# Speech codec kernel, one core: two halo rows copied instead of loaded, x by two eight-row transposes a chunk, fewer DMA adds, three small copies and two updates on other engines

## The chip, the cores and the metric

One core of a Trainium2 chip runs the whole program. The metric is device microseconds of one execution, as the median of three runs. Beside the runs stands one profiled execution, whose trace is read below.

## What is computed

The input x is 2 sequences of 16,000 tokens with 512 channels, in bf16. The reference, cut to what matters:

```python
z = sum over i of xp[:, i:i+T, :] * dw_enc[i]      # 3 taps along the tokens, x padded by one row
z = silu(z)
res = z; q = zeros_like(z)
for s in range(4):                                  # 4 stages, 8 code words each
    cb = codebooks[s]
    d2 = |res|^2 - 2 * res @ cb.T + |cb|^2
    sel = cb[d2.argmin(-1)]
    q = q + sel
    res = res - sel
y = sum over i of qp[:, i:i+T, :] * dw_dec[i]      # 3 taps again
```

So every token needs itself and its two neighbours, then four rounds of "score against 8 words, take the least, subtract the word", and the output is made from the words chosen for a token and its neighbours.

## The kernel before

The 32,000 tokens are dealt over 128 partitions: partition p holds 250 consecutive tokens. Column g of that grid is one "group" of 128 tokens. The 250 groups are worked in 17 chunks, one of 12 groups, thirteen of 16, then 12, 12 and 6 (padded to 8). Within a chunk channels stand on the partitions: x comes in transposed, as the tile XT of 128 channels by (groups + 2) by 4 channel blocks by 128 tokens.

A chunk passes through three parts:

- **Front** (`front`, and `load` ahead of it). `load` brings XT in with DMA transposes on SyncE's queue (L507), four rows (groups) a DMA. A chunk of 16 groups needs 18 rows, because the taps reach one group to either side; so it takes five DMAs, of 4, 4, 4, 4 and 2 rows, and neighbouring chunks load two rows twice. XT has two buffers. For each of the four channel blocks i, VectorE multiplies by the three taps (`product`, L578) into the tiles Z, T1 and T2; then T1 and T2 are added to Z (`total`). An addition is either a VectorE instruction (L586) or an accumulating DMA that GpSimd issues (L584); the table `DMA_ADDS` says which. The result goes through SiLU: exp on ScalarE (L590), plus one on VectorE (L594), reciprocal on ScalarE (L599), a product on VectorE into the residual RES (L606).
- **Four stages** (`stage`). TensorE scores RES against the words (L680, with a mask at L672). VectorE reduces the scores to a maximum that holds the token's norm (L700), ScalarE copies out the products (L706), and four VectorE instructions (L733 to L748) find the least distance and mark it in OH. TensorE turns the marks (L759), the turned marks are copied from PSUM to the tile MT, TensorE expands them (L784) and ScalarE cuts them into PH (L793). The table `TURNED` says who makes the MT copy: VectorE in the first three stages (L775), ScalarE in the fourth (L773). Then the word is taken off RES, channel block by channel block. Either TensorE makes the chosen word (`chosen`, L822) and VectorE adds it (`subtract`, L832), or TensorE makes the whole new residual in PSUM (`rest`, L838 and L843) and ScalarE copies it back in two halves (`keep`, L850). The table `ON_DVE` gives, for each chunk and stage, how many of the four blocks take VectorE's way.
- **Finish** (`finish`, `outputs`). TensorE multiplies the marks with tables of words times taps (L886), ScalarE copies the rows out of PSUM into YSB (L896), and SyncE's queue stores them, four groups a DMA (L899). YSB has two buffers.

Three chunks are in work at a time (RES has three buffers). The order of everything is a plan: each piece of work is a task with an engine, a holding time, a delay, needs and buffers, and the string `RANKS` gives each task its start in the plan, by which the instructions are emitted; `PLACES` gives the PSUM banks. The engines then run their queues strictly in that order, each waiting on semaphores.

One rule is written by hand: transposes and accumulating DMAs take turns. `keep_apart` makes each transpose wait for the last add but one that was emitted before it, and each add for the last transpose but one (`LAG = 2`).

```python
    def keep_apart(t, mine, others):
        if len(others) >= LAG:
            tc.add_manual_dep(t.ins, others[-LAG].name, mybir.DependencyInfo(mybir.DependencyClass.Sync, mybir.DependencyReason.DATA),
                              reason="transposes and adds take turns")
        mine.append(t.ins)
```

So SyncE's queue, which holds transposes and stores in one order, can stand at a transpose until an add has landed, with stores behind it; GpSimd's queue can stand at an add until a transpose has landed.

Of the kernel before, what the change touches and what calls it, by code (L numbers as in the profile page):

```python
# [18 lines left out]
J = 4  # L19
# [10 lines left out]
TURNED = (0, 0, 0, 1)  # L30

ON_DVE = [(3, 3, 3), (3, 3, 3), (3, 3, 3), (3, 3, 3), (3, 2, 3), (3, 3, 3), (3, 2, 3), (3, 3, 3), (3, 2, 3), (3, 3, 3), (3, 2, 3), (3, 3, 3), (3, 2, 3), (3, 3, 3), (4, 4, 4), (4, 4, 4), (4, 4, 4)]
# [5 lines left out]
DMA_ADDS = [((), ())] + [((0, 1, 2, 3), (2, 3))] * 16  # L38

RUN = 4  # L40
# [8 lines left out]
RANKS = ("0403020v1u1W0i1A0J0E0O0U0x0k3`4e4t4p4M4A523<0z001o1F1+1|1T1-1D1V5Q01121E1)1c252x01051G5]001!5$0f1Q1w5*0a1c1m5-1(1|2Y1-2]"  # L49
         "323Q2r2w2K2T2/3h3.22282i2d2B3w3U1]1=312*3g3L3)3!43404k4L4!4!4<4{5f5l575q5w5G5O5Z5(5+5[5^606A6J6b6m656d6q6Q6g6J6I6-6_7l6Y"  # L50
         "6?7k7x7F7S7#7&7;7>7_8b8r7~87858h8N8!8s8D8Z8>959c8*8^9b9i9l9n9t9w9D9F9Ma4ak9X9)9R9^9$9~agaxasaJa%a?aYa]b8bobMcvcWc(c=dod&"
         "d|d,d?eKf@g2d,eqfqgNgZeGeTiGe`fijkjC4d3p4o5j5v5I5;4`3C5f4,5{687c393Z3[3v4>6r6S4G3J4P5I5;6Z766?7m7n7H7G7%7Z7^8B8S8Y8g8z8K"
         "8X8+9d9j9m9q9v9y9E9J9R9`a9aqaLa9at9:a6axa,aLb7bwbLa[b4bsb0bkbrbZb*b<b|c0c5c8cfcAc!cucJclcxcTc*cHcVc*d0dednc>dadmdadwd%d."
         "d`d}eLeXe;e>fbfiftfpfGfIfUfPf$fwfKf$f[g4gng3ghgsgSg<hdhVh%h<h|ioiziFiWi$i`j5i-i@jojAj:jhjqjZk3jCjLjXjHjOj_khkRkuk!l4lm2:"
         "3S3q2:5H3c6Y6~7t8E8W8,9c7<6(7}6/8.9e9x7y6w7!8L8`9-a37V6C8q8}9safaFaEa-a@bababBbtbNb)b]b}b>c7ccb!b?b^ctcUcXc.c;c@dhdHeket"
         "d{e6dWd:dMeBd)e9eseMe(e]e*e^fge!e-e[fsfFfRf)g1g9gegng@h5gGgRg/g_g#g;gwgQg~hBhOh,hrhEh$hihzh%h{h~ibiriui.i=j0jsjGj9jnjBjR"
         "jTj)k0kskbk#k~l7kBkUl8lelslAlLlZl$l*l.m3mqmImOmVm:n#n>oSo&qjmPm&o1qBmOoDo@oeoromozp[n=n|pEq95P8R6h716O6=9M9Ga(9!cbcndTb+"
         "9=c6b!c]d4dqbpaWbAb}cCdodZa|9Tb9cmc&dLd(d*eiejeMe$e}e^fhgkg?hcf!f?glf:f_gthghphwhChLhThWh&i3ieiaiCihirh[i8h.h~iqi!i@i~iP"
# [54 lines left out]
LAG, SLACK, STORE = 2, 4.5, 0.35  # L113
# [61 lines left out]
def kernel(  # L175
# [318 lines left out]
    def load(st, org):  # L494
# [30 lines left out]
        def behind():  # L525
            nc.gpsimd.tensor_copy(st["XT"][0:1, 0, 0, 0:2], XR[0:1, 1, 0:2])
            nc.gpsimd.tensor_copy(st["XT"][0:1, 0, 0, 2:4], CB4[0:1, 0:2])
            for b in range(B):
                p = b * HB + 32
                nc.gpsimd.tensor_copy(st["XT"][p:p + 1, 0, 0, 0:2], XR[p:p + 1, 0, 0:2])  # L530
# [492 lines left out]
```

## Time and profile before

| what | value |
|---|---|
| median of 3 runs | 687.65 us (678.28 to 690.9) |
| the profiled execution, its own time | 681.25 us |
| its span, first to last instruction | 679.5 us |
| mean granted TensorE clock | 0.936 |
| VectorE busy | 605.9 us (89%) |
| ScalarE busy | 555.2 us (82%) |
| TensorE busy with matmuls | 537.8 us (79%) |
| DMA moved | 119.38 MB |

The profile's page gives for each engine the busy time, its share of the span and the number of instructions. DVE is VectorE, ACT ScalarE, PE TensorE (PEld its weight loads), POOL GpSimd, SP SyncE; a "q" behind a name is the engine's sequencer, which issues and waits. A group of instructions is named by line, engine, operation and tiles (out<-in); behind the bar stand its busy time, the mean of one in ns, and the idle time of the engine just before them with what ended it. A row of the view of waits reads: who waited, at which line, for whom, total us, number of waits, longest. The view of windows gives each engine's busy time within a stretch, then the granted clock, the DMA share (mean busy share of the 16 DMA engines; it can pass 1 where packets overlap) and GB/s.

### The profile page before, as it was taken

Reading aid. Unit: us, or ns where it says so; the run is one execution under the profiler, and the core shown is the slowest. Engines: PE = TensorE matmul, PEld = TensorE weight load, DVE = VectorE, ACT = ScalarE, POOL = GpSimd, SP = SyncE. Lnnn points to the kernel's source line nnn. Section 1 sums busy time; section 2 is a strip of 40 time slices with the busy share of each in tenths; the row PEclk is TensorE's granted clock in tenths of the full one; section 3 lists DMA queues with packets and bytes.
Section 4 is the critical chain, followed back from the end, with each engine's and each line's share of the span. In section 5 each row is a group of like instructions: output and inputs, shape, how many; then the busy total and the mean of one; then the engine's idle time right before and its main releaser. Section 6 shows DMA issues by size and latency. Waiting matters only on the chain.

```text
span 679.5 us, 25822 instructions
## 1 busy us (share of the span) xinstructions
PE 537.8 (79%) x11513; PEld 324.4 (48%) x11550; DVE 605.9 (89%) x1166; ACT 555.2 (82%) x675; POOL 102.1 (15%) x147
## 2 busy tenths in 40 slices
PE   4136686788888697887988979579879998899995
PEld 4123345355455444454454544345545555566661
DVE  5998999999999698998889999499979999999961
ACT  2567586979798699998899988499969889997586
POOL 8020203011212102020211102012120122110000
PEclk8657799989899799998999999899989999999998
DMA  8999899979999999999999997989979487362345
GB/s 166 161 181 193 145 174 179 187 157 166 242 223 178 154 213 180 229 175 184 224 185 210 167 249 137 130 211 184 204 152 184 118 155 187 88 163 91 127 170 204
DMA packets 164889, 119.38 MB, mean 176 GB/s; under 512 B 143801, under 2 KB 144186, under 8 KB 164650
## 3 DMA queue, kind: packets, MB, share of 16 engines
q1 hardware_dynamic: 150032, 69.88, 49.2%
q0 software_dynamic: 14464, 47.59, 38.7%
q8 instruction: 90, 1.47, 0.9%
q10 hardware_dynamic: 282, 0.26, 0.1%
q14 instruction: 21, 0.17, 0.1%
HBM read 2.36 MB, written 32.77 MB: 52 GB/s over the span
## 4 chain that ended last, share of the span: by engine, by line
DVE 40%; ACT 18%; PE 16%; DMA 15%; issue 9%; POOL 1%; SPq 0%; ACTq 0%; DVEq 0%; POOLq 0%
DVE RES L832 11%; DMA XT<-in_x_dram 8%; DVE T L578 6%; PE PS L680 6%; DVE TR L700 6%; DMA Z<-T 5%; DVE RES L606 5%; ACT E L599 5%; PE PS L822 4%; ACT E L590 4%; ACT YSB L896 4%; DVE E L594 3%; DVE Z L578 3%; ACT RES L850 2%; DVE Z L586 2%
## 5 line engine op out<-in xcount | busy, mean ns | idle before, releaser
L680 PE MATMUL PS<-RES 128*64 128x80 bf16 (+1 forms) x8064 | 177.1, 202 | 36.3 <-issue 25.4
L680 PEld LDWEIGHTS <-RES 128*64 128x64 bf16 x8064 | 171.5, 114 | 45.2 <-issue 26.7
L832 DVE TENSOR_TENSOR RES<-RES,PS 128x2048 bf16<-128x2048 bf16 (+2 forms) x202 | 175.6, 902 | 10.3 <-PE PS L822 9.8
L584 POOL DMA_DIRECT2D Z<-T x96 | 85.9, 944 | 498.8 <-DVE TR L700 70.7
L896 ACT ACTIVATE YSB<-PS 128x1024 bf16<-128x1024 f32 x126 | 124.0, 1031 | 13.6 <-PE PS L886 8.6
L590 ACT ACTIVATE E<-Z 128x2048 bf16<-128x2048 bf16 (+2 forms) x68 | 121.3, 1792 | 13.0 <-DVE Z L586 11.3
L599 ACT ACTIVATE E<-E 128x2048 bf16<-128x2048 bf16 (+2 forms) x68 | 121.7, 1799 | 1.1 <-DVE E L594 0.9
L700 DVE TENSOR_REDUCE TR<-PS 128x6 bf16<-128x384 f32 (+1 forms) x188 | 93.9, 509 | 17.4 <-PE PS L680 14.6
L578 DVE TENSOR_SCALAR T<-XT,WENC 128x2048 bf16<-128x2048 bf16 (+2 forms) x136 | 94.9, 710 | 11.9 <-DMA XT<-in_x_dram 10.7
L850 ACT ACTIVATE RES<-PS 128x1024 bf16<-128x1024 f32 x88 | 89.9, 1032 | 7.4 <-PE PS L843 6.9
L606 DVE TENSOR_TENSOR RES<-Z,E 128x2048 bf16<-128x2048 bf16 (+2 forms) x68 | 77.6, 1141 | 1.3 <-ACT E L599 1.3
L706 ACT ACTIVATE PR<-PS 128x48 bf16<-128x48 f32 (+1 forms) x188 | 36.0, 215 | 49.2 <-DVE TR L700 48.9
L822 PE MATMUL PS<-PH,HIGH 64*128 64x512 bf16 (+2 forms) x314 | 62.2, 381 | 12.2 <-ACT PH L793 4.2
L672 PE MATMUL PS<-MASK,IDENT 128*64 128x384 bf16 (+1 forms) x376 | 63.1, 327 | 11.0 <-ACT RES L850 4.6
L838 PE MATMUL PS<-RES,IDENT 128*128 128x512 bf16 (+1 forms) x188 | 58.1, 391 | 4.7 <-DVE RES L832 2.0
L822 PE MATMUL PS<-PH,LOW 64*128 64x512 bf16 (+2 forms) x314 | 59.7, 366 | 0.4 <-issue 0.4
L822 PE MATMUL PS<-PH,MID 64*128 64x512 bf16 (+2 forms) x314 | 59.7, 366 | 0.1
L886 PE MATMUL PS<-S,OHT 64*128 64x512 bf16 (+1 forms) x169 | 53.4, 397 | 6.1 <-DVE RES L832 2.7
L886 PE MATMUL PS<-T,OHT 64*128 64x512 bf16 (+1 forms) x170 | 51.9, 395 | 5.5 <-ACT OHT L790 1.8
L578 DVE TENSOR_SCALAR Z<-XT,WENC 128x2048 bf16<-128x2048 bf16 (+2 forms) x68 | 48.3, 710 | 5.6 <-DMA XT<-in_x_dram 5.3
L672 PEld LDWEIGHTS <-IDENT 128*64 128x64 bf16 x376 | 24.9, 109 | 44.5 <-issue 41.2
L586 DVE TENSOR_TENSOR Z<-Z,T 128x2048 bf16<-128x2048 bf16 (+2 forms) x40 | 44.2, 1112 | 0.8 <-DMA Z<-T 0.8
(109 smaller groups left out, 594.4 us busy)
## 6 DMA issues: line engine op xcount, KB each, us to landing
Z<-T POOLq DMA_DIRECT2D x78, 512.0 KB, 6.7
out_dram<-YSB SPq DMA_DIRECT2D x61, 512.0 KB, 4.6
Z<-T POOLq DMA_DIRECT2D x12, 384.0 KB, 5.8
RES<-in_x_dram SPq DMA_DIRECT2D x1, 1664.0 KB, 7.1
Z<-T POOLq DMA_DIRECT2D x6, 256.0 KB, 4.5
XT<-in_x_dram SPq DMA_TRANSPOSE x76, 6.4
out_dram<-YSB SPq DMA_DIRECT2D x1, 384.0 KB, 2.3
out_dram<-YSB SPq DMA_DIRECT2D x1, 256.0 KB, 2.6
```

Of the source, the lines that this page charges most:

```text
L578: nc.vector.tensor_scalar(out=places(u[name]), in0=taps(i, k), scalar1=WENC[:, i, k:k + 1], scalar2=None, op0=ALU.mult)
L590: nc.scalar.activation(u["E"][:, 0:G, :], u["Z"][:, 0:G, :], ACT.Exp, scale=-1.0)
L599: nc.scalar.add_instruction(mybir.InstActivation(func=ACT.Reciprocal, name=nc.get_next_instruction_name(), engine=mybir.EngineType.Activation,
L606: nc.vector.tensor_tensor(out=tokens(st["RES"], i, G), in0=halves(u["Z"]), in1=halves(u["E"]), op=ALU.mult)
L672: nc.tensor.matmul(both(V[d * HT:(d + 1) * HT], m, home, HT), lhsT=IDENT[:, d * HT:(d + 1) * HT], rhs=MASK[:, 0:m, :].rearrange("p (n o) t ...
L680: nc.tensor.matmul(V[d * HT:(d + 1) * HT, own - left:own + HT + right], lhsT=row[:, at:at + HT], rhs=row[:, at - left:at + HT + right], st ...
L700: nc.vector.tensor_reduce(out=to, in_=both(u["V", q], m, home, HT), axis=AX.X, op=ALU.max)
L822: nc.tensor.matmul(SEL[:, h, 0:W], lhsT=words[side(h), i * P:(i + 1) * P], rhs=u["PH"][side(h), :], start=(k == 0), stop=(k == len(parts) ...
L832: nc.vector.tensor_tensor(out=old, in0=old, in1=new, op=ALU.add)
L850: nc.scalar.activation(old, new.rearrange("p h (n t) -> p (h n) t", t=HT), ACT.Copy)
L886: nc.tensor.matmul(Y[:, h, :], lhsT=lhs()[rows], rhs=DEC[table][rows], start=(a == 0), stop=(a == len(banks[k][h][1]) - 1), skip_group_che ...
L896: nc.scalar.activation(u["YSB"][:, at:at + step * (n - 1) + 1:step, :], u[k][:, 0:n, :], ACT.Copy)
```

## The change

Five things change in the code, and the plan's tables are new throughout.

- `load`: rows 0 and 1 of XT are no longer loaded. A new task `halo` lets VectorE copy them from the last two rows of the XT of the chunk before (L535 of the changed kernel). `RUN` goes from 4 to 8, so a chunk of 16 groups takes two transposes of eight rows.
- The XT buffer used to come free with the last `product` of its chunk. Now a new task `released` frees it when that product and the next chunk's halo copy are both done.
- `DMA_ADDS`: in the even chunks from 2 to 16 the second addition of channel block 2 goes from DMA to VectorE. Of 96 accumulating DMAs 88 are left.
- `TURNED`: the MT copies of the first three stages, 51 of them, go from VectorE to ScalarE.
- `ON_DVE`: chunks 1, 3, 5, 7, 9, 11 and 13 have (3, 2, 3), before it was chunks 4, 6, 8, 10 and 12. So two more chunks have one more channel block that goes through `rest` and `keep`.

The holding times and delays that the plan gives to transposes, adds and stores are other numbers, too, and stand in the diff.

```diff
-TURNED = (0, 0, 0, 1)
+TURNED = (1, 1, 1, 1)
-ON_DVE = [(3, 3, 3), (3, 3, 3), (3, 3, 3), (3, 3, 3), (3, 2, 3), (3, 3, 3), (3, 2, 3), (3, 3, 3), (3, 2, 3), (3, 3, 3), (3, 2, 3), (3, 3, 3), (3, 2, 3), (3, 3, 3), (4, 4, 4), (4, 4, 4), (4, 4, 4)]
+ON_DVE = [(3, 3, 3), (3, 2, 3), (3, 3, 3), (3, 2, 3), (3, 3, 3), (3, 2, 3), (3, 3, 3), (3, 2, 3), (3, 3, 3), (3, 2, 3), (3, 3, 3), (3, 2, 3), (3, 3, 3), (3, 2, 3), (4, 4, 4), (4, 4, 4), (4, 4, 4)]
-DMA_ADDS = [((), ())] + [((0, 1, 2, 3), (2, 3))] * 16
-RUN = 4
+DMA_ADDS = [((), ()), ((0, 1, 2, 3), (2, 3)), ((0, 1, 2, 3), (3,)), ((0, 1, 2, 3), (2, 3)), ((0, 1, 2, 3), (3,)), ...]
+RUN = 8
-RANKS = ("0403020v1u1W0i1A0J0E0O0U0x0k3`4e4t4p4M4A523<0z001o1F1+1|1T1-1D1V5Q01121E1)1c252x01051G5]001!5$0f1Q1w5*0a1c1m5-1(1|2Y1-2]"
+RANKS = ("0303020v1u1W0i1A050f010U0x0k3}4k4%4U5A4J5S4U0z001T1-1o1F1D1V1+1|6f013i121@1c020O1c6Y0a1G6%0J1w1Q6u0E1m1!6N2w222K282Y2+3l"
...
-LAG, SLACK, STORE = 2, 4.5, 0.35
+LAG, STORE = 2, 0.35
...
+        last = chunks[st["n"] - 1]
+
+        def halo():
+            nc.vector.tensor_copy(st["XT"][:, 0:2, :, :], last["XT"][:, last["G"]:last["G"] + 2, :, :])
+
         room = plan.add("SP", 0.0, 0.0, [], org - 2.2 * PERIOD, place, take=("XT",))
+        st["halo"] = plan.add("DVE", 0.33, 0.45, [room] + last["loaded"], org - 0.5 * PERIOD, halo)
...
-        for n in range(0, G + 2, RUN):
+        for n in range(2, G + 2, RUN):
             due = org - 2.2 * PERIOD + 0.01 * n
             m = min(RUN, inside - n)
             if m > 0:
-                done.append(plan.add("DMA", 0.7 * m, SLACK + 0.1 + 0.7 * m, [room], due, lambda n=n, m=m: run(n, m), mode=RUNS))
+                done.append(plan.add("DMA", 0.86 * m, 2.7 + 0.86 * m, [room], due, lambda n=n, m=m: run(n, m), mode=RUNS))
...
-        st["loaded"] = done + [st.get("edge")]
+        st["loaded"] = done + [st["halo"], st.get("edge")]
...
-                    return plan.add("DMA", 0.1 + 2.65 * f, SLACK + 2.65 * f, needs, due, lambda: total(k), give=("T",), mode=ADDS)
+                    return plan.add("DMA", 0.1 + 2.75 * f, 3.7 + 2.75 * f, needs, due, lambda: total(k), give=("T",), mode=ADDS)
...
-            t = plan.add("DVE", hold, delay, here + (st["taps"] if i == KT - 1 else []), due, lambda: product(2), take=("T",), give=("XT",) if i == KT - 1 else ())
+            t = plan.add("DVE", hold, delay, here + (st["taps"] if i == KT - 1 else []), due, lambda: product(2), take=("T",))
...
-                landed.append(plan.add("DMA", STORE * n, 0.4 + STORE * n, part, due, lambda at=stored, n=n: store(at, n)))
+                landed.append(plan.add("DMA", STORE * n, 3.2 + STORE * n, part, due, lambda at=stored, n=n: store(at, n)))
...
+    def released(st, after):
+        plan.add("FREE", 0.0, 0.0, [st["taps"][-1], after["halo"]], 0.0, lambda: None, give=("XT",))
```

What that does to the queues is seen at three places. First SyncE's queue in the middle of the run, before; XT is the turned input of a chunk, YSB the output rows, and the middle number of a transpose is its rows times four channel blocks:

```order
L507 DMA_TRANSPOSE XT<-in_x_dram 128x16x128 x2
L899 DMA out_dram<-YSB 128x2048
L507 DMA_TRANSPOSE XT<-in_x_dram 128x16x128
L507 DMA_TRANSPOSE XT<-in_x_dram 128x8x128
L899 DMA out_dram<-YSB 128x2048 x3
L507 DMA_TRANSPOSE XT<-in_x_dram 128x16x128 x2
L899 DMA out_dram<-YSB 128x2048 x2
L507 DMA_TRANSPOSE XT<-in_x_dram 128x16x128
L899 DMA out_dram<-YSB 128x2048 x2
```

and SyncE's queue there with the change:

```order
L905 DMA out_dram<-YSB 128x2048 x3
L507 DMA_TRANSPOSE XT<-in_x_dram 128x32x128 x2
L905 DMA out_dram<-YSB 128x2048 x2
L507 DMA_TRANSPOSE XT<-in_x_dram 128x32x128
L905 DMA out_dram<-YSB 128x2048 x2
L507 DMA_TRANSPOSE XT<-in_x_dram 128x32x128
L905 DMA out_dram<-YSB 128x2048 x2
```

The five pieces of a chunk have become two, each as long as two of the old ones, and the stores stand behind and between them as before.

Second, VectorE's queue in the middle of the run, before; T is a product that is to be added to Z, OH the marks of a stage, MT their turned copy:

```order
L743 TENSOR_REDUCE M<-KEY_125 128x16
L700 TENSOR_REDUCE TR<-PS 128x6
L748 TENSOR_TENSOR OH_128<-KEY_125,M 128x128
L586 TENSOR_TENSOR Z<-Z,T_7488 128x2048
L832 TENSOR_TENSOR RES_88<-RES_88,PS 128x2x16x64 x2
L775 COPY MT<-PS 128x128
L700 TENSOR_REDUCE TR<-PS 128x6
```

and with the change, where the XT of chunk 12 gets its halo from that of chunk 11 and a second addition of chunk 10 is done:

```order
L592 TENSOR_TENSOR Z<-Z,T_7113 128x2048
L749 TENSOR_REDUCE M<-KEY_127 128x16
L584 TENSOR_SCALAR T_7665<-XT,WENC 128x2048
L754 TENSOR_TENSOR OH_128<-KEY_127,M 128x128
L600 TENSOR_SCALAR E<-E 128x2048
L584 TENSOR_SCALAR T_7677<-XT,WENC 128x2048
L706 TENSOR_REDUCE TR<-PS 128x6
L535 COPY XT<-XT 128x1024
L584 TENSOR_SCALAR T_7707<-XT,WENC 128x2048
```

The marks OH are no longer followed by an MT copy on this queue, and the halo copy stands among the products of chunk 11, whose rows it copies.

Third, ScalarE's queue in the same part of the run with the change:

```order
L596 ACTIVATE E<-Z 128x2048
L799 ACTIVATE PH<-PS 128x512
L902 ACTIVATE YSB<-PS 128x2x512
L779 ACTIVATE MT<-PS 128x128
L596 ACTIVATE E<-Z 128x2048
L799 ACTIVATE PH<-PS 128x512
L712 ACTIVATE PR<-PS 128x8x6
```

The MT copy now stands between long instructions of ScalarE, here an output copy and an exp, and the PH of the same stage, which needs that copy, comes behind the exp.

More of the change, by code (lines that the diff above doesn't have):

```diff
@@ L985 @@
             load(st, org)
+            released(chunks[st["n"] - 1], st)
         front(st, org)
+        if st["n"] == 0:
+            released(st, chunks[1])
         for s in range(Nq):
```

113 lines of the change are left out of this document (57 added, 56 removed).

## The prediction

> **What bounds the kernel now.** I read the page first, then the windows, the waits, and last the chain and single instructions.
>
> ```profile
> span 679.5 us, 25822 instructions
> PE 537.8 (79%) x11513; PEld 324.4 (48%) x11550; DVE 605.9 (89%) x1166; ACT 555.2 (82%) x675; POOL 102.1 (15%) x147
> DMA  8999899979999999999999997989979487362345
> DMA packets 164889, 119.38 MB, mean 176 GB/s; under 512 B 143801, under 2 KB 144186, under 8 KB 164650
> q1 hardware_dynamic: 150032, 69.88, 49.2%
> q0 software_dynamic: 14464, 47.59, 38.7%
> HBM read 2.36 MB, written 32.77 MB: 52 GB/s over the span
> ```
>
> VectorE has the most work, 605.9 of 679.5 us. But the 16 DMA engines are busy nine tenths in most slices of the first three quarters, too: SyncE's queue (q1, transposes and stores) fills 49.2% of them and the accumulating DMAs (q0) 38.7%. Two things are nearly full at once. The windows say which of them costs time; the columns are stretch, length, busy us of PE, PEld, DVE, ACT and POOL, clock, DMA share, GB/s.
>
> ```profile
> 0.00:80.00 80.00, 34.46 (x403) 22.84 (x403) 69.01 (x148) 44.91 (x40) 23.38 (x57) 0.68 0.98 168
> 80.00:600.00 520.00, 433.91 (x9622) 259.03 (x9651) 480.97 (x857) 452.47 (x543) 77.59 (x89) 0.97 0.95 181
> 600.00:680.00 80.00, 69.39 (x1490) 42.51 (x1496) 55.91 (x163) 57.85 (x93) 1.16 (x1) 0.96 0.39 150
> ...
> 400.00:440.00 40.00, 28.56 (x692) 18.31 (x693) 29.79 (x53) 29.07 (x39) 4.37 (x5) 0.94 0.99 141
> 440.00:480.00 40.00, 35.93 (x732) 20.22 (x735) 39.44 (x71) 37.71 (x43) 5.64 (x6) 0.98 1.00 198
> 560.00:600.00 40.00, 34.68 (x842) 22.28 (x844) 39.90 (x84) 39.54 (x52) 8.71 (x10) 1.00 0.61 137
> ```
>
> VectorE's idle time is 11.0 us in the start, 39.0 us between 80 and 600 us, and 24.1 us in the end. Only the middle can react to this change: the start waits for its first loads, and the end works off the last chunks with the DMA at 0.39. Where the DMA share is 0.61 (560 to 600 us), VectorE and ScalarE both run at 99%. Where it is 0.99 or 1.00, VectorE did as little as 29.8 of 40 us, or as much as 39.4. So VectorE is the bound and a full DMA is what throws it off. The waits name it:
>
> ```profile
> DVE TR L700 <- PE PS L680: 11.0, 11, 2.1
> DVE T L578 <- DMA XT<-in_x_dram: 10.7, 2, 8.6
> DVE Z L578 <- DMA XT<-in_x_dram: 5.3, 2, 4.1
> DVE RES L832 <- PE PS L822: 5.1, 6, 1.6
> ...
> ACT PR L706 <- DVE TR L700: 32.8, 32, 8.4
> ```
>
> These are the waits between 80 and 600 us. The largest single cause is the turned input: 16.0 us in four waits. The longest of them in the chain of waits:
>
> ```profile
> 416.71 5.62 DMA Z<-T
> 422.33 0.02 issue
> 422.35 15.66 DMA XT<-in_x_dram
> ```
>
> A transpose could not start before an add had landed, and then took 15.66 us to come in, while VectorE stood still for 8.56 us of it. That is the taking of turns plus a full set of DMA engines. SyncE's queue shows how common it is:
>
> ```profile
> SPq L507 <- DMA Z<-T: 219.1, 24, 17.9
> ```
>
> **The change, part by part.** Durations are from the profiled execution, so the sum stands against its own time, 681.25 us (span 679.5 and 1.75 around it). The median of the three runs, 687.65, lies 6.4 us higher.
>
> *VectorE's work.* The rows and, for how closely instructions follow each other, a piece of the order of time:
>
> ```profile
> L832 DVE TENSOR_TENSOR RES<-RES,PS 128x2048 bf16<-128x2048 bf16 x112 | 134.8, 1215 | 5.4 <-PE PS L822 5.1
> L586 DVE TENSOR_TENSOR Z<-Z,T 128x2048 bf16<-128x2048 bf16 x26 | 31.7, 1218 | 0.8 <-DMA Z<-T 0.8
> L775 DVE COPY MT<-PS 128x128 bf16<-128x128 bf16 x51 | 10.8, 217 | 0.0
> L284 DVE COPY RES<-CBT 128x1024 bf16<-128x1024 bf16 x3 | 1.3, 421 | 0.0
> L372 DVE TENSOR_SCALAR RES<-HIGH 128x512 uint16<-128x512 uint16 x3 | 0.9, 286 | 0.0
> ```
>
> ```profile
> 298.53 1.21 DVE L832 TENSOR_TENSOR RES<-RES,PS 128x2048 bf16<-128x2048 bf16 x1
> 299.66 0.22 DVE L748 TENSOR_TENSOR OH<-KEY,M 128x128 bf16<-128x128 bf16 x1
> 299.80 1.21 DVE L832 TENSOR_TENSOR RES<-RES,PS 128x2048 bf16<-128x2048 bf16 x1
> 300.93 0.22 DVE L775 COPY MT<-PS 128x128 bf16<-128x128 bf16 x1
> 301.06 0.41 DVE L700 TENSOR_REDUCE TR<-PS 128x4 bf16<-128x256 f32 x1
> ```
>
> Starts follow each other 0.08 us sooner than the durations say, so a full add or update holds VectorE 1.13 us and an MT copy 0.13 us. Eight second additions come to VectorE, six full ones and two of shorter chunks, which I take by their size: 6 x 1.13 + 0.87 + 0.60 = +8.3 us. Sixteen halo copies of 128x1024: the trace has none between two XT tiles, and the nearest rows give 0.29 us (half the size) and 0.42 us. I take the row of its own size, 0.42, of which 0.34 holds the engine: 16 x 0.34 = +5.4 us (3.3 to 6.7). The MT copies go: -51 x 0.13 = -6.6 us (-11.1 by their full duration). Two updates go: -2.3 us. Together **+4.8 us** (-2 to +6). VectorE gets no lighter. As it is the bound, this counts in full.
>
> *The DMA engines' work.* Eight adds less, six of 512 KB, one of 384 and one of 256, take 3.7 MB off 47.6, so 3.0 of q0's 38.7 points. Two of 18 rows less take a ninth off the transposes. By bytes these have 37.1 of q1's 69.9 MB (the rest is what is written), 26 points; by packets nearly all, 47. So 2.9 to 5.2 points go. The total falls from 89% by 6 to 8 points, about a twelfth, and the 0.95 of the middle to about 0.88.
>
> *The size of a transpose.* The rows of the transposes and of their issues:
>
> ```profile
> DMA to landing us min/median/max: 4.2/6.4/15.1
> XT<-in_x_dram SPq DMA_TRANSPOSE x76, 6.4
> ```
>
> Four rows land in 6.4 us at the median. Eight rows lie between that and twice it; with 9.6, two of them take 19 us where five took up to 32 one after the other, and fewer of the turns between transposes and adds remain: 32 transposes where there were 76. One transpose, though, now keeps the adds away for twice as long. Behind each on SyncE's queue stand stores, and behind these the two YSB buffers of ScalarE; that wait has cost little so far:
>
> ```profile
> L896 ACT ACTIVATE YSB<-PS 128x1024 bf16<-128x1024 f32 x126 | 124.0, 1031 | 13.6 <-PE PS L886 8.6 <-PE PS L822 2.2 <-DMA out_dram<-YSB 1.4
> ```
>
> The Trainium skill, "DMA: Bandwidth & Descriptors", section "Anatomy of one DMA", gives a DMA about 2.0 us fixed and its bytes at 436 GB/s, so an estimated 3.2 us for 512 KB and 4.4 us for 1 MB. The trace's fastest transpose took 4.2 us, a third more than the page's figure for its size. By the page's figures the turned input would never be late again and the sum would be 663 instead of 665 us.
>
> *What VectorE regains.* Of the 16.0 us of waits for XT I take 14 off: a transpose of eight rows can still run into an add, as at 422 us. Of the other 23 us of the middle I take a third, 7 us: waits for TensorE that follow behind a late input. **-21 us** (0 to -39).
>
> *ScalarE's work.* The nearest rows for an MT copy of 128x128 out of PSUM, one half of an update, and an exp:
>
> ```profile
> L706 ACT ACTIVATE PR<-PS 128x48 bf16<-128x48 f32 x128 | 26.1, 218 | 35.6 <-DVE TR L700 35.6
> L773 ACT ACTIVATE MT<-PS 128x256 bf16<-128x256 bf16 x1 | 0.4, 415 | 0.0
> L850 ACT ACTIVATE RES<-PS 128x1024 bf16<-128x1024 f32 x88 | 89.9, 1032 | 7.4 <-PE PS L843 6.9
> L590 ACT ACTIVATE E<-Z 128x2048 bf16<-128x2048 bf16 x52 | 99.5, 1918 | 4.5 <-DVE Z L586 3.0 <-DMA Z<-T 1.3
> ```
>
> Between 218 and 415 ns I take 300: 51 x 0.30 + 4 x 1.03 = +19.4 us (15 to 25), some 17 of it in the middle. There ScalarE was idle 67.5 of 520 us, so I cost it at nothing. If that cover is gone it costs up to 17 us. The copy also waits its turn behind exps of 1.9 us, and TensorE's expansion, PH and VectorE's next update wait for it; two other chunks give these engines work meanwhile.
>
> *TensorE* gets two blocks of the costlier kind, some 3 us of its 142 idle: nothing. The halo copy itself waits for a neighbour that landed a chunk earlier, and the XT buffer is freed only after it; its place among the neighbour's products makes that no later than the last product.
>
> **Sum:** 681.25 + 4.8 - 21 = 665 us in the profiled execution's terms. Two of the three runs lie above that execution, by 6.4 and 9.6 us; I take late transfers for the cause and keep half of the median's 6.4: **668 us**, 2.9% under 687.65.
>
> **Rivals.**
>
> *A, the stalls only move.* An eight-row transpose holds the adds off for twice as long, and VectorE waits for Z where it waited for XT. For it: the turns stay as they were, and the waits of SyncE for adds are 219.1 us. Against it: VectorE waited only 0.8 us for an add to Z, by the row of L586. Price: nothing regained, +4.8: 686 in the profiled terms, up to 692 as a median.
>
> *B, ScalarE becomes the bound (slower).* Place: ScalarE's queue in the middle. Its 67.5 us of idle time there is half waits for VectorE's maxima (32.8 us), which come in order and do not shrink when ScalarE gets more to do. If all of it stays, the middle takes 452.5 + 17 + 67.5 = 537 us: 698 us, as a median up to 704. It decides once ScalarE's idle time in the middle stays above 50 us. Against it: at 560 to 600 us both engines ran at 99%.
>
> *C, the middle runs as 560 to 600 us did.* VectorE's 480.97 + 4.8 at 99.75% take 487 us, 33 less: 648, as a median 651. Against it: the DMA share would still be 0.9, not 0.61.
>
> **How the numbers follow.** My forecast 0.50, with 655 to 680 us as its own range; A 0.22; B 0.15; C 0.13. A measurement of this kernel tells about 2% from no change: below 673.9 us is faster, above 701.4 us slower by the median shown. About a seventh of the forecast's range lies above 673.9. So faster is 0.43 + 0.13 = 0.56. Same is 0.07, A, and the part of B below its full price, 0.04: 0.33. Slower is the rest of B, 0.11. The range 645 to 694 us leaves out the upper half of B and the lower half of C.
>
> **What would show it.** Right: the DMA share of the middle under 0.92; no wait of VectorE for XT over 3 us; VectorE's busy time 608 to 613 us with its idle time in the middle under 25 us; ScalarE's busy time 570 to 580 us. Wrong: VectorE waits for Z or XT for over 10 us in all (A), or its waits for TensorE grow while ScalarE's idle time in the middle falls below 35 us (B). A busy time of VectorE above 616 us would make the sum itself wrong.

## The result, and the profile after

The changed kernel takes 722.83 us (median of four runs, 715.57 to 733.32) where the kernel before, run beside it, takes 684.82 (678.28 to 690.9). The ratio is 1.061 (95% interval 1.054 to 1.068): slower by 6%, against a forecast of 3% faster and outside the range. The profiled execution took 723.45 us.

The head of the page of the changed kernel:

```profile
span 721.7 us, 25767 instructions
PE 557.1 (77%) x11561; PEld 326.4 (45%) x11561; DVE 612.2 (85%) x1137; ACT 570.3 (79%) x730; POOL 97.3 (13%) x139
DMA  9779398988979996959989975959567693523344
DMA packets 145944, 111.37 MB, mean 154 GB/s; under 512 B 125881, under 2 KB 126266, under 8 KB 145706
q1 hardware_dynamic: 132240, 65.68, 41.3%
q0 software_dynamic: 13312, 43.79, 33.6%
```

VectorE's work rose by 6.3 us, ScalarE's by 15.1, and 8 MB less were moved. The span rose by 42.2 us, so 35.9 of these are new idle time of VectorE. The windows (stretch, length, then PE, PEld, DVE, ACT, POOL, clock, DMA share, GB/s) say where:

```profile
0.00:80.00 80.00, 39.85 (x562) 26.81 (x564) 68.67 (x148) 47.40 (x46) 21.34 (x54) 0.70 0.85 155
80.00:640.00 560.00, 445.74 (x9469) 256.11 (x9465) 482.79 (x829) 460.94 (x580) 72.53 (x81) 0.93 0.80 156
640.00:722.00 82.00, 71.56 (x1552) 43.43 (x1544) 60.77 (x162) 61.96 (x105) 3.43 (x4) 0.98 0.41 143
```

In the middle VectorE is idle 77.2 us, before 39.0; the start (11.3) is as it was and the end (21.2) is 2.9 us shorter of idle time. The DMA share fell from 0.95 to 0.80, further than the 0.88 of the forecast, and yet the middle takes longer. The waits of VectorE between 80 and 640 us:

```profile
DVE T L584 <- DMA Z<-T: 31.1, 8, 14.7
DVE TR L706 <- PE PS L686: 22.1, 22, 3.5
DVE RES L838 <- PE PS L828: 9.3, 9, 4.9
DVE E L600 <- ACT E L596: 7.2, 6, 4.0
...
DVE Z L592 <- DMA Z<-T: 0.9, 1, 0.9
```

No wait for XT is left: 16.0 us became nothing. In its place stand 31.1 us in which a product (L584) waits for a buffer T that an accumulating DMA still reads; that wait was 0.2 us before, the last figure of this row of the kernel before:

```profile
L578 DVE TENSOR_SCALAR T<-XT,WENC 128x2048 bf16<-128x2048 bf16 (+2 forms) x136 | 94.9, 710 | 11.9 <-DMA XT<-in_x_dram 10.7 <-ACT XT L481 0.8 <-DMA Z<-T 0.2
```

The waits for TensorE (TR and RES) nearly doubled, from 16.1 to 31.4 us. TensorE's granted clock in the middle fell from 0.97 to 0.93; which part of these longer waits comes from that and which from late inputs is not shown. The waits for ScalarE's exp (E) are new, 7.2 us where there were 0.3; the exps themselves waited 7.2 us for accumulating DMAs. The longest piece of the chain of waits is such a DMA:

```profile
235.62 0.49 issue
236.11 27.87 DMA Z<-T
264.00 0.75 DVE T L584
```

The two issuing queues there, first SyncE's, then GpSimd's (start, length of the issue, instruction):

```profile
235.27 10.45 SPq L507 DMA_TRANSPOSE XT<-in_x_dram  x1
247.97 0.81 SPq L905 DMA_DIRECT2D out_dram<-YSB  x2
248.87 19.96 SPq L507 DMA_TRANSPOSE XT<-in_x_dram  x1
```

```profile
235.53 1.72 POOL L590 DMA_DIRECT2D Z<-T  x2 [9.13 <-DVE T L584]
```

A transpose of eight rows begins at 235.27, and two adds are issued 0.26 and 0.84 us later. `LAG = 2` allows that: an add waits for the last transpose but one. VectorE then stands still twice, until the first of the two adds has landed and until the second has:

```profile
245.57 0.75 DVE L584 TENSOR_SCALAR T<-XT,WENC 128x2048 bf16<-128x2048 bf16 x1 [6.20 <-DMA Z<-T]
...
264.00 0.75 DVE L584 TENSOR_SCALAR T<-XT,WENC 128x2048 bf16<-128x2048 bf16 x1 [14.73 <-DMA Z<-T]
```

What the DMA engines did meanwhile, by the windows, and by the DMA view of 245 to 260 us and of 267 to 270 us (the adds have landed by 263.98):

```profile
245.00:260.00 15.00, 2.10 (x19) 1.19 (x19) 3.70 (x8) 5.07 (x7) 0.00 (x0) 0.50 1.24 57
```

```profile
DMA packets 1582, 0.86 MB, mean 57 GB/s; under 512 B 1464, under 2 KB 1464, under 8 KB 1581
q1 hardware_dynamic: 1449, 0.37, 83.2%
q0 software_dynamic: 132, 0.48, 39.3%
```

```profile
DMA packets 3281, 0.84 MB, mean 280 GB/s; under 512 B 3281, under 2 KB 3281, under 8 KB 3281
```

This is the place to learn from; below it is called the accident. The share is 1.24, "more than full", and 57 GB/s get through, though from 245.57 us on only the second of the two adds is still under way; once the adds are gone a transpose alone moves 280. So a high share does not show that bytes get on. Between 230 and 270 us VectorE is idle for 24.0 us, out of 77.2 in the whole middle; the rest is spread over many shorter waits.

### The profile page after: what moved, and what is told of

It is laid out like the page before. It is cut to its first block, busy times and chain, and to the rows that moved or that the text cites. A ratio compares the mean times of both kernels' runs of the same rounds, so it can differ in the third digit from the quotient of the medians.

```text
span 721.7 us, 25767 instructions
## 1 busy us (share of the span) xinstructions
PE 557.1 (77%) x11561; PEld 326.4 (45%) x11561; DVE 612.2 (85%) x1137; ACT 570.3 (79%) x730; POOL 97.3 (13%) x139
## 4 chain that ended last, share of the span: by engine, by line
DVE 29%; PE 28%; ACT 19%; DMA 13%; issue 10%; ACTq 0%; POOL 0%; DVEq 0%; POOLq 0%
DMA Z<-T 11%; PE PS L686 9%; DVE RES L838 8%; PE PS L828 6%; ACT YSB L902 5%; DVE RES L612 4%; DVE T L584 4%; ACT E L605 4%; PE PS L892 4%; DVE Z L592 3%; ACT E L596 3%; DVE TR L706 3%; DVE Z L584 3%; ACT RES L856 3%; PE PS L678 2%
## 5 line engine op out<-in xcount | busy, mean ns | idle before, releaser
L686 PE MATMUL PS<-RES 128*64 128x72 bf16 (+1 forms) x8064 | 181.7, 204 | 26.9 <-issue 23.3
L838 DVE TENSOR_TENSOR RES<-RES,PS 128x2048 bf16<-128x2048 bf16 (+2 forms) x200 | 172.0, 896 | 14.4 <-PE PS L828 13.7
L590 POOL DMA_DIRECT2D Z<-T x88 | 80.9, 951 | 553.1 <-DVE Z L584 108.2
L584 DVE TENSOR_SCALAR T<-XT,WENC 128x2048 bf16<-128x2048 bf16 (+2 forms) x136 | 95.0, 706 | 31.8 <-DMA Z<-T 31.1
L856 ACT ACTIVATE RES<-PS 128x1024 bf16<-128x1024 f32 x92 | 93.8, 1042 | 5.3 <-PE PS L849 5.0
L844 PE MATMUL PS<-RES,IDENT 128*128 128x512 bf16 (+1 forms) x196 | 61.5, 393 | 13.4 <-DVE RES L838 6.6
L892 PE MATMUL PS<-T,OHT 64*128 64x512 bf16 (+1 forms) x187 | 56.4, 393 | 3.4 <-ACT OHT L796 1.2
L892 PE MATMUL PS<-S,OHT 64*128 64x512 bf16 (+1 forms) x186 | 56.5, 388 | 2.2 <-ACT YSB L902 1.1
L592 DVE TENSOR_TENSOR Z<-Z,T 128x2048 bf16<-128x2048 bf16 (+2 forms) x48 | 52.8, 1110 | 0.9 <-DMA Z<-T 0.9
L828 PEld LDWEIGHTS <-HIGH 64*128 64x128 bf16 x310 | 22.7, 106 | 59.9 <-issue 47.7
L600 DVE TENSOR_SCALAR E<-E 128x2048 bf16<-128x2048 bf16 (+2 forms) x68 | 43.4, 645 | 7.2 <-ACT E L596 7.2
```

The lines of the kernel that those rows point to most:

```text
L584: nc.vector.tensor_scalar(out=places(u[name]), in0=taps(i, k), scalar1=WENC[:, i, k:k + 1], scalar2=None, op0=ALU.mult)
L590: keep_apart(nc.gpsimd.dma_start(out=z, in_=t, accum_op=ALU.add), adds, runs)
L686: nc.tensor.matmul(V[d * HT:(d + 1) * HT, own - left:own + HT + right], lhsT=row[:, at:at + HT], rhs=row[:, at - left:at + HT + right], st ...
L828: nc.tensor.matmul(SEL[:, h, 0:W], lhsT=words[side(h), i * P:(i + 1) * P], rhs=u["PH"][side(h), :], start=(k == 0), stop=(k == len(parts) ...
L838: nc.vector.tensor_tensor(out=old, in0=old, in1=new, op=ALU.add)
L856: nc.scalar.activation(old, new.rearrange("p h (n t) -> p (h n) t", t=HT), ACT.Copy)
```

## The experiments

Five theories. T: a transpose of eight rows and adds under way at the same time slow each other down, so that both come late. M: the MT copy on ScalarE lengthens the stages. V: the adds that came to VectorE are what is missed. H: the halo copy ties one chunk to the next. P: the new order as such. All ratios are to the kernel before, run beside the kernel on the same chip.

**One part of the change undone.** In the changed kernel: MT copies back on VectorE (a1); strict turns, where a transpose waits for the last add and an add for the last transpose (a2); each eight-row transpose cut into two of four, back to back (a3). In the kernel before: MT copies to ScalarE (a4).

```diff
a1, after
-TURNED = (1, 1, 1, 1)
+TURNED = (0, 0, 0, 1)
a2, after
-LAG, STORE = 2, 0.35
+LAG, STORE = 1, 0.35
a3, after
-            t = nc.sync.dma_start_transpose(...)
-            keep_apart(t, runs, adds)
+            for a in range(0, m, 4):
+                b = min(4, m - a)
+                t = nc.sync.dma_start_transpose(out=st["XT"][:, n + a:n + a + b, :, :]..., in_=xv[:, g + a:g + a + b, :]...)
+                keep_apart(t, runs, adds)
a4, before
-TURNED = (0, 0, 0, 1)
+TURNED = (1, 1, 1, 1)
```

> The changed kernel (722.83 us) with the 51 MT copies back on VectorE, in the same places of the plan. Theory T, transfers collide: eight-row transposes that overlap with adds slow both, so VectorE waits for T buffers that an add still holds; MT plays no part: 715 to 726 us, VectorE's waits for adds stay above 20 us. Rival M, the MT copy in ScalarE's queue lengthens every stage and VectorE waits for TensorE: 695 to 708 us, VectorE's waits for TensorE fall by 12 us or more. Rival P, the new order as such (its delays of adds and transposes are too short): 715 to 726 us.

Measured: 721.0 us, ratio 1.060 (1.047 to 1.072). M falls for the changed kernel: it gains nothing by the copies back on VectorE.

> The changed kernel with LAG = 1: each transpose waits for the last add and each add for the last transpose, so the two kinds never overlap. Theory T: 690 to 710 us, no landing over 14 us after the start of the run, VectorE's waits for adds below 15 us. Rival M: 718 to 728 us. Rival P: slower than the changed kernel, 725 to 740 us, since every add and transpose is later still.

Measured: 695.42 us, ratio 1.022 (1.010 to 1.035): 27 of the 38 us come back by this one number. The waits of VectorE there, 80 to 620 us:

```profile
DVE T L584 <- DMA Z<-T: 14.7, 9, 4.0
```

The waits are as many, but none is over 4.0 us.

> The changed kernel with each transpose of eight rows cut into two of four, one right behind the other in the same place. The rule of turns then lets an add overlap with four rows at most. Theory T, if the size is what hurts: 695 to 712 us. Rival M: 718 to 728 us. Rival P: 715 to 728 us.

Measured: 705.38 us, ratio 1.034 (1.021 to 1.048): 17 us come back by cutting the transposes alone. The rule of turns counts pieces, so an add now also meets four rows at most.

> The kernel before (684.82 us) with its 51 MT copies on ScalarE, all else and the order unchanged. Theory T and rival P: 682 to 690 us. Rival M: 697 to 708 us, with VectorE's waits for TensorE up by 12 us or more.

Measured: 687.86 us (675.93 to 693.55) where the kernel before had 684.63. The median is 0.5% over it, but the four runs spread over 18 us, so this run says little.

**One part of the change alone.** The kernel before with strict turns (b1); the changed kernel with all 96 DMA adds (b2); the kernel before with the halo copy and transposes of four rows, so four a chunk instead of five (b3); the same with two transposes of eight rows, in the places of the first and the third piece (b4).

```diff
b1, before
-LAG, SLACK, STORE = 2, 4.5, 0.35
+LAG, SLACK, STORE = 1, 4.5, 0.35
b2, after
-DMA_ADDS = [((), ()), ((0, 1, 2, 3), (2, 3)), ((0, 1, 2, 3), (3,)), ...]
+DMA_ADDS = [((), ())] + [((0, 1, 2, 3), (2, 3))] * 16
b3 (ROWS_AT_ONCE = 4) and b4 (8), before
...
+        def piece(n):
+            m = min(ROWS_AT_ONCE, inside - n - 2)
+            if m > 0 and n % ROWS_AT_ONCE == 0:
+                run(n + 2, m)
+            if n + RUN >= min(G + 2, inside):
+                nc.vector.tensor_copy(st["XT"][:, 0:2, :, :], last["XT"][:, last["G"]:last["G"] + 2, :, :])
...
-                done.append(plan.add("DMA", ..., lambda n=n, m=m: run(n, m), mode=RUNS))
+                done.append(plan.add("DMA", ..., lambda n=n: piece(n), mode=RUNS))
```

> The kernel before (684.6 us) with LAG = 1, so that transposes and adds never overlap. Theory T (overlap between the two kinds slows both, and it hurts in proportion to the size of a transpose): with four-row pieces the overlap is small and there are many turns, so little change: 676 to 692 us. Rival P (what the strict rule cured in the changed kernel was something of its order alone): no gain here, 690 to 710 us, since more turns are waited out.

Measured: 741.86 us, ratio 1.088 (1.080 to 1.097). Theory T, as I had put it, misses here: with five pieces a chunk the overlap of transposes and adds is worth far more than it costs.

> The changed kernel (722 us) with the eight second additions back on DMA, 96 accumulating DMAs as before, all else and the order unchanged. Theory T: more adds that can meet an eight-row transpose: 720 to 740 us. Rival V (VectorE's extra 8.3 us of additions is part of the loss): 708 to 716 us.

Measured: 750.12 us, ratio 1.097 (1.084 to 1.111). V falls: giving VectorE eight adds helped the changed kernel, by 3.6% of the time before or some 25 us. That is more than T had expected, too (720 to 740 us).

> The kernel before with the halo part alone: rows 0 and 1 of XT copied by VectorE from the neighbour's XT, the other rows by four-row transposes in the places that they had in the order (four pieces a chunk instead of five). Theory T: a ninth less of transposes, four-row pieces as before: 674 to 686 us. Rival H (the halo copy ties chunks together and delays VectorE or the release of XT): 692 to 710 us.

Measured: 678.12 us, ratio 0.995 (0.990 to 1.000). H falls for the order before: the halo copy with its two rows less costs nothing there. It is the best version of this study, and not surely better than before.

> As the run with the halo alone, but with two transposes of eight rows, in the places of the first and the third piece; the order of everything else is that of before. Theory T, that the size of a transpose by itself brings the collisions: 695 to 715 us, with adds and transposes that land after more than 15 us. Rival P, that the new order brings them: within 1% of the run with the halo alone, 676 to 690 us.

Measured: 713.37 us, ratio 1.048 (1.038 to 1.058). The eight rows alone cost 35 us against b3, in the order before. P is not needed for the greater part. The same accident shows in b4's trace, though with the order before; its SyncE queue, its GpSimd queue, and the windows:

```profile
342.94 13.76 SPq L508 DMA_TRANSPOSE XT<-in_x_dram  x1
```

```profile
343.14 1.78 POOL L594 DMA_DIRECT2D Z<-T  x2 [4.65 <-DVE T L588]
```

```profile
345.00:360.00 15.00, 9.40 (x172) 4.75 (x170) 7.04 (x15) 10.32 (x14) 0.00 (x0) 0.89 1.26 93
360.00:372.00 12.00, 0.00 (x0) 0.00 (x0) 0.84 (x2) 0.00 (x0) 0.00 (x0) 0.50 1.13 116
```

A transpose of eight rows, two adds 0.2 and 0.8 us behind it, a share of 1.26 at 93 GB/s; TensorE and ScalarE do nothing for 12 us, and VectorE waits, by its row among the waits:

```profile
DVE T L588 <- issue: 18.4, 1, 18.4
```

That the releaser is called "issue" only says that the profile saw none; the wait ends as the add lands (issued at 343.72, it took 27.06 us). The other wait that grew is that for XT, 21.0 us in b4 and 7.5 in b3; first two rows of b4, then two of b3:

```profile
DVE T L588 <- DMA XT<-in_x_dram: 17.2, 2, 8.8
DVE Z L588 <- DMA XT<-in_x_dram: 3.8, 1, 3.8
```

```profile
DVE Z L588 <- DMA XT<-in_x_dram: 4.5, 2, 3.1
DVE T L588 <- DMA XT<-in_x_dram: 3.0, 2, 2.0
```

So in this one trace about 18 us of the loss are the accident, and some 13 are turned input that comes late.

**Halves of the explanation.** b3 with the 88 DMA adds of the change (c1); b4 with strict turns (c2); the changed kernel with strict turns for the adds alone (c3); and with each eight-row transpose as two of four, the second 3.5 us later in the plan (c4).

```diff
c1, b3
-DMA_ADDS = [((), ())] + [((0, 1, 2, 3), (2, 3))] * 16
+DMA_ADDS = [((), ()), ((0, 1, 2, 3), (2, 3)), ((0, 1, 2, 3), (3,)), ...]
c2, b4
-LAG, SLACK, STORE = 2, 4.5, 0.35
+LAG, SLACK, STORE = 1, 4.5, 0.35
c3, after
-        if len(others) >= LAG:
-            tc.add_manual_dep(t.ins, others[-LAG].name, ...
+        lag = 1 if mine is adds else LAG
+        if len(others) >= lag:
+            tc.add_manual_dep(t.ins, others[-lag].name, ...
c4, after
...
+                h = min(4, m)
-                done.append(plan.add(..., lambda n=n, m=m: run(n, m), mode=RUNS))
+                done.append(plan.add(..., lambda n=n, h=h: run(n, h), mode=RUNS))
+                if m > h:
+                    second.append((done[-1], lambda n=n, h=h, m=m: run(n + h, m - h)))
...
+        plan.apart.append((at, 3.5))
```

> The kernel before with the halo copy alone (four transposes of four rows a chunk, 678.12 us) and with eight DMA adds less as in the change (88 instead of 96). Theory T (only overlap of long transposes with adds makes DMA adds dear): with four-row transposes few adds collide, so eight adds less save little and VectorE's 8.3 us more count: 675 to 692 us. Rival R (eight DMA adds less are worth as much here as in the changed kernel, where they were worth 27 us): 650 to 668 us.

Measured: 691.12 us, ratio 1.012 (1.004 to 1.020). With four rows eight DMA adds less cost 1.7% against b3, some 12 us, and VectorE's busy time rises from 610.7 to 618.6 us. R falls.

> The kernel before with two transposes of eight rows a chunk in its own order (713.37 us) and with strict turns (LAG 1: no transpose starts while an add is under way, and no add while a transpose is). Theory T: the overlap goes, and with two pieces a chunk there are few turns, so 685 to 700 us. Rival (strict turns cost as much as with five pieces a chunk, 57 us, and eight rows are slow by themselves): 720 to 745 us.

Measured: 706.54 us, ratio 1.038 (1.030 to 1.045), between the two. In this order strict turns give back at most some 7 of the 35 us, and the two intervals overlap. Whether the rest is waiting for turns or the longer single transfer by itself, this run does not tell.

> The changed kernel in which only the adds take strict turns: an add waits for the last transpose emitted before it, while a transpose still waits for the last add but one. Theory T with adds started on transposes as the overlap that hurts: 690 to 702 us, most of what strict turns on both sides gave (695.42). If the overlap that hurts is that of transposes started on adds: 712 to 725 us.

Measured: 715.82 us, ratio 1.050 (1.043 to 1.058), inside the second range. Holding back the adds alone is not enough. That transposes started on adds hurt as much fits this, but the run with the transposes alone held back was not made.

> The changed kernel with each eight-row transpose cut into two of four rows, the second of them 3.5 us later in the plan than the first, so that adds can stand between. Theory T (the size of one transpose is what costs): 680 to 698 us, further down than the two halves back to back (705.38). Theory P (the new order as such costs, whatever the size): 700 to 712 us.

Measured: 701.43 us, ratio 1.032 (1.025 to 1.039): no better than back to back (705.38), by a little P's case. Two per cent over c1, which has the same adds and the same sizes, remain with the new order and the work moved to ScalarE.

**The transfers by themselves.** d1 leaves out everything the reference computes and only runs transposes and accumulating DMAs, 8 MB of a kind in each stage; the first figure of a stage is the number of transfers of a kind under way at a time, N8 is 8 and N4 and NADD are 16. With four rows, two more tests of what bounds the kernel: b3 with eight DMA adds more (d2), and with the MT copies on ScalarE (d3).

```diff
d1, in place of the whole program
+        stage(1, (turn8, N8))
+        stage(1, (turn4, N4))
+        stage(1, (add, NADD))
+        stage(1, (turn8, N8), (add, NADD))
+        stage(1, (turn4, N4), (add, NADD))
+        stage(2, (turn8, N8), (add, NADD))
+        stage(2, (turn4, N4), (add, NADD))
d2, b3
-DMA_ADDS = [((), ())] + [((0, 1, 2, 3), (2, 3))] * 16
+DMA_ADDS = [((), ())] + [((0, 1, 2, 3), (2, 3) if n % 2 else (1, 2, 3)) for n in range(1, 17)]
d3, b3
-TURNED = (0, 0, 0, 1)
+TURNED = (1, 1, 1, 1)
```

> The transfers by themselves, with none of the computation: seven stages one after the other, each of 8 MB of transposes (eight of eight rows or sixteen of four) or 8 MB of accumulating DMAs (sixteen of 512 KB) or both side by side; first with one transfer of a kind under way at a time, last with two. The kernel leaves out everything the reference computes. Theory T: side by side with adds, eight-row transposes take longer than both would one after the other (stage of both at least 1.2 times the sum of the two stages alone), and four-row ones clearly less than that. Rival S (the overlap costs nothing by itself; the two share the DMA engines fairly, and what hurts in the kernel is only the longer single wait): both side by side take no more than the sum of the two alone, and eight rows and four rows agree within 10%.

Measured, as windows from the first issue of a stage to the end of its last transfer (columns: stretch, length, VectorE, GpSimd, clock, DMA share, GB/s), in the order of the diff, and last a piece out of the sixth stage:

```profile
0.70:48.90 48.20, 3.65 (x4) 0.00 (x0) 1.00 0.78 174
48.90:116.50 67.60, 0.00 (x0) 0.00 (x0) 1.00 0.58 124
117.10:193.85 76.75, 0.00 (x0) 13.91 (x16) 1.00 0.57 109
193.90:294.30 100.40, 0.00 (x0) 13.77 (x16) 1.00 0.93 167
294.30:393.25 98.95, 0.00 (x0) 13.77 (x16) 1.00 0.95 170
393.30:517.30 124.00, 0.00 (x0) 13.81 (x16) 1.00 1.19 135
517.40:608.95 91.55, 0.00 (x0) 13.79 (x16) 1.00 1.11 183
398.00:446.00 48.00, 0.00 (x0) 2.67 (x4) 1.00 1.28 76
```

One of each side by side is a gain with either size (100.4 and 98.95 us, where one after the other takes 125.0 and 144.4). With two of each, four rows take less still (91.55), and eight rows more than with one of each: 124.0, and 48 us of it at a share of 1.28 and 76 GB/s. The low rate of the kernel's accident comes back with nothing else running. Both theories miss in part: against the stages with one at a time, T's 1.2 times is not reached (124.0 against 125.0), and S is refuted by the 35% between the sizes.

> The kernel before with the halo copy alone (678.12 us), four-row transposes, and eight DMA adds more (104 instead of 96: the second addition of block 1 in the even chunks goes from VectorE to DMA). If VectorE's work is what counts there, as eight adds less cost 12 us: 665 to 674 us. If the DMA engines (share 0.95) cannot take more: 680 to 700 us.

Measured: 714.72 us, ratio 1.060 (1.051 to 1.070). Eight adds more on the DMA cost 6.5% against b3, although VectorE's busy time falls from 610.7 to 606.0 us. That is beyond the second range, too.

> The kernel before with the halo copy alone (678.12 us), four-row transposes, and all MT copies on ScalarE. If VectorE's work is what counts: 6.6 us less on it, so 668 to 676 us. If ScalarE's longer copy lengthens the stages: 678 to 690 us.

Measured: 689.84 us, ratio 1.022 (1.013 to 1.031), 2.7% over b3, though VectorE's busy time fell from 610.7 to 607.0 us. In this order M holds. In a4, without the halo copy, the same move shows a median of only 0.5% more.

**Which depth it is.** e1 repeats d1 with other depths. e2 and e3 are the changed kernel with the adds, or the transposes, one at a time.

```diff
e1, number under way at a time as third figure
+        stage((turn8, N8, 2))
+        stage((turn4, N4, 2))
+        stage((add, NADD, 2))
+        stage((turn8, N8, 1), (add, NADD, 2))
+        stage((turn8, N8, 2), (add, NADD, 1))
+        stage((turn8, N8, 2), (add, NADD, 2))
+        stage((turn8, N8, 2), (add, NADD, 2))
+        stage((turn4, N4, 2), (add, NADD, 2))
+        stage((turn4, N4, 2), (add, NADD, 2))
+        stage((turn4, N4, 1), (add, NADD, 2))
e2 (adds) and e3 (runs), after
+        if mine is adds and mine:
+            tc.add_manual_dep(t.ins, mine[-1].name, ..., reason="one at a time")
         mine.append(t.ins)
```

> The transfers by themselves again (nothing of what the reference computes), to tell which depth makes two kinds side by side slow. Ten stages of 8 MB of a kind: eight rows, two under way; four rows, two; adds, two; then side by side eight rows one and adds two, eight two and adds one, eight two and adds two, that again, four rows two and adds two, that again, four rows one and adds two. In the first run of this kind eight rows two with adds two took 124 us, eight rows one with adds one 100, four rows two with adds two 92, and within the 124 lay 48 us at 76 GB/s. Theory T (an eight-row transpose beside adds collapses when the transfers queue up): both stages of eight rows two with adds two take 115 to 135 us, and the eight-row stages with only one of a kind doubled lie between 95 and 125; four rows two with adds two stay at 85 to 97. If the 124 us was an accident of one stage: its repetitions take 90 to 100 us, as four rows do.

Measured, the ten stages in order:

```profile
0.74:37.80 37.06, 3.65 (x4) 0.00 (x0) 1.00 1.07 226
37.87:82.90 45.03, 0.00 (x0) 0.00 (x0) 1.00 0.99 186
83.09:130.01 46.92, 0.00 (x0) 13.93 (x16) 1.00 0.95 179
130.06:269.52 139.46, 0.00 (x0) 13.78 (x16) 1.00 1.03 120
269.59:364.10 94.51, 0.00 (x0) 13.76 (x16) 1.00 0.91 178
364.11:505.30 141.19, 0.00 (x0) 13.81 (x16) 1.00 1.18 119
505.33:641.95 136.62, 0.00 (x0) 13.78 (x16) 1.00 1.17 123
641.98:755.60 113.62, 0.00 (x0) 13.78 (x16) 1.00 1.14 148
755.61:883.75 128.14, 0.00 (x0) 13.78 (x16) 1.00 1.18 131
883.78:999.80 116.02, 0.00 (x0) 13.78 (x16) 1.00 0.94 145
```

It was not the chance of one stage. Eight rows beside two adds take 139.5, 141.2 and 136.6 us, whether one or two transposes are under way; one kind after the other takes 37.1 + 46.9 = 84.0 with two transposes at a time, and 48.2 (d1) + 46.9 = 95.1 with one. Beside one add at a time they take 94.5 us, and of these the last 38 are adds alone. So in these stages the long loss comes with two adds at once, and one transpose is enough; in the kernel's accident the low rate lasted on when the first of the two adds had landed. Four rows are not safe from it: two and two take 113.6 and 128.1 here, where d1 had 91.55, against 92.0 one after the other; one and two take 116.0 against 67.6 (d1) + 46.9 = 114.5. They lose less. None of T's ranges held: eight rows with two adds lost more than it said, two transposes with one add at a time came out just under theirs, and four rows were not spared.

> The changed kernel with the adds one at a time (each waits until the add before it has landed); nothing else. If two adds at once beside an eight-row transpose make the collapse: 690 to 710 us. If not, the adds only come later: 723 to 745 us.

Measured: 860.22 us, ratio 1.254 (1.243 to 1.265), far beyond both cases. The plan lives on two adds at a time; one at a time, VectorE waits for them all through the run:

```profile
DVE T L587 <- DMA Z<-T: 116.2, 26, 13.5
```

So this run cannot tell what the adds' depth costs in the kernel; e1 tells it only for the transfers by themselves.

> The changed kernel with the transposes one at a time (each waits until the transpose before it has landed); nothing else. If two eight-row transposes at once make the collapse: 695 to 712 us. If one is enough beside adds: 715 to 730 us.

Measured: 725.71 us, ratio 1.058 (1.050 to 1.066). One eight-row transpose is enough, as in e1: the accident stands at the same place in e3's trace, with a transpose issued at 232.09 us, two adds 0.3 us later, and an add that lands only after 25.9 us.

## Why the prediction was wrong

*The bound.* VectorE was named as the bound, with the full DMA as what throws it off. Half of that stands. c1 fits VectorE's side: eight adds taken from the DMA cost some 12 us, where the sum had 8.3. d2 shows the other: eight adds given to it cost 6.5%. In its own order the kernel before stands where both moves cost, and the one towards the DMA costs more; neither run had its plan made anew.

*VectorE's work, +4.8 us.* About right: +6.3. The halo copies took 417 ns each, as taken.

*The DMA engines' work.* Right as a count (8.0 MB less, share 0.80 to 0.82 in the middle) and useless as an argument. A falling share was taken for room. In the lost stretches the share is over 1 and the bytes are few.

*The size of a transpose: the step that failed.* "One transpose, though, now keeps the adds away for twice as long" was said and costed at nothing. The duration was right (9.6 us taken, 9.1 measured at the median). (That median is over the transposes whose landing the trace tells.) What failed is the picture behind it, of transfers that keep each other away and take turns. `LAG = 2` lets them run side by side, and where an eight-row transpose met two adds both went slowly: an add of 512 KB landed in 27.87 us, and alone one takes 4.8 (d1: 76.75 / 16). The size alone costs 35 us in the order before (b4 against b3). In the changed kernel four rows back to back give 17 us back, strict turns 27. The prediction saw the symptom in the trace before, the transpose that took 15.66 us at 422 us, and read it as "a full set of DMA engines".

Eight rows took 6.0 us alone (d1: 48.20 / 8). By the Trainium skill, "DMA: Bandwidth & Descriptors", section "Anatomy of one DMA", which the prediction weighed, 1 MB takes an estimated 4.4 us. That section measured DMAs issued by GpSimd, and the transposes here are SyncE's. The sum by that section, 663 us, was further off than the prediction's own. The Trainium skill, same page, section "Rules for kernel authors", says that a transpose next to ordinary DMAs needs nothing. That row is about lost data; in time, beside accumulating DMAs, e1 shows a cost (139.5 us where one after the other takes 95.1).

*What VectorE regains, -21 us.* The waits for XT went, as forecast, from 16.0 to 0. But the adds' 31.1 us, TensorE's extra 15.3 (TR and RES) and 6.9 more for the exps took their place, and the middle's idle time went up by 38.2 instead of down by 21. In the terms of the profiled executions, 723.45 against a sum of 665, the miss is 58 us: this step alone makes 59, VectorE's work another 1.5, and start and end gave 2.6 back.

*ScalarE's work, +19.4 us at no cost.* Busy time +15.1. In the changed kernel it cost nothing (a1). In b3's order the same move cost 2.7% (d3), so "idle time covers it" held by luck of the order. That a short copy on a queue of long ones is a matter of when more than of how much is a reading of these two runs, not tested by itself.

*The rivals.* A had the place and nearly the wait: adds that come late. Its sign, over 10 us of waits for Z or XT, did not come by the letter (0.9 us for Z, none for XT), because the 31.1 us are waits for the buffer T that a late add still reads. Its price was at most 692: it let the stall move without growing. Nothing in it asked what two transfers do to each other. B's sign is there, ScalarE's idle time in the middle is 99.1 us (560 - 460.94) and so above 50; but a1 takes ScalarE's extra copies away and gains nothing, and a2, which leaves them, gains 27 us. C is refuted by the time.

*The signs and the chances.* Four of the five signs that were to show the forecast right came: a DMA share under 0.92 (0.80), no long wait for XT, VectorE busy for 612.2 us, ScalarE for 570.3. Only VectorE's idle time in the middle, 77.2 us where it should be under 25, spoke against it. And of the forecast's own range, 655 to 680 us, a quarter lies above 673.9, not a seventh; with a quarter the chance of faster would have been about 0.51.

*What stays open.* Why two adds at once do this to a transpose, and why four rows fell into it in e1 and not in d1. Why the low rate lasts on beside one add in the kernel. How much of b4's 35 us is slowed transfers and how much the longer single wait: c2, without overlap, gets at most 7 back, and what it pays for its turns cannot be parted from that. What makes the last 2% of c4. The seven `ON_DVE` entries were not tried alone. The parts do not add: halo, eight rows, fewer adds and MT copies, each by itself, come to 1 - 0.5% + 5.3% + 1.7% + 2.7% = 1.092, and together they gave 1.061 in their own order.

## What to carry to other kernels

When a change makes transfers fewer and larger, ask first what else is under way beside them, and look in the trace for a stretch where the DMA share is over 1 while the GB/s fall: in these runs that was the price of a meeting, and it was higher for eight rows than for four. Read load from GB/s, and share only together with it. A stall that moves is to be priced anew at its new place, with the duration that the transfer has there, not with what it cost where it stood.

## What the runs showed of the hardware

- Accumulating DMAs two at a time move 179 GB/s, one at a time 109. Eight-row transposes: 226 and 174; four-row ones: 186 and 124. Beside one add at a time the two sizes took the same (100.4 and 98.95 us), and beside two adds, within each run, eight rows took longer than four.
- Eight-row transposes beside two adds: 119 to 135 GB/s over whole stages, 76 over 48 us, each at a share over 1; in the kernel 57 over 15 us at a share of 1.24, with one of the two adds still under way.
- TensorE's granted clock stood at 0.50 where TensorE had stood nearly still (245 to 260 us in the changed kernel, 360 to 372 us in b4), and over the middle at 0.93 where it was 0.97 before.
- The issue of a transpose is long when this happens: 10.45 and 19.96 us on SyncE's queue in the changed kernel, and what stands behind it on that queue waits too.
